# FFN products as two streams of 64 array rows, one on w_in and one on w_out

## The chip, the cores and the metric

The kernel runs on one core of one Trainium2 chip. A core has five engines that run side by side, each through its own instructions in order: TensorE (PE, matrix products into the accumulation memory PSUM), VectorE (DVE) and ScalarE (ACT) for elementwise work, GpSimd (POOL), and SyncE (SP), which here issues the DMA transfers. The profile counts TensorE's loads of stationary operands as an engine of their own, PEld. PSUM has eight banks; a bank holds 128 partitions x 512 float32. The metric is the time of one execution on the device in microseconds (us); lower is better.

## The reference, cut to what matters

Two parts follow each other. The first is attention with decay over 4 sequences of 768 tokens, 8 heads of 64. The second takes its result, 3072 tokens x 512, through a feed-forward network (FFN) whose nonlinearity is a ratio of two polynomials:

```python
for t in range(S):
    state = gamma * state + einsum('bhd,bhe->bhde', k[:, :, t], v[:, :, t])
    y[:, :, t] = scale * einsum('bhd,bhde->bhe', q[:, :, t], state)
x = y.transpose(0, 2, 1, 3).reshape(3072, 512)
h = x @ w_in                                  # 512 -> 2048
P = a[0] + a[1] * h + a[2] * h * h + a[3] * h * h * h
Q = 1.0 + abs(b[0]) * abs(h) + abs(b[1]) * h * h
out = (P / (Q + 1e-06)) @ w_out               # 2048 -> 512
```

## The kernel before, in words

**Blocks and slots.** The tokens are cut into 6 blocks of 512. Attention makes a block as four chunks of 128 tokens. The 2048 hidden features are cut into 16 tiles of 128. A *slot* is one pair (block n, feature tile f); `order` lists the 96 of them: blocks 0 and 1 with tiles 0 to 7, both again with tiles 8 to 15, then blocks 2 to 5 with 16 tiles each. Each FFN operand is held as a rounded high part and a low part, and a product takes three terms: high x high, high x low, low x high.

**One slot on PE.** `gemm_in` (L346) makes h for the slot in one PSUM bank `ph` (two banks take turns) with 12 products: three terms by four parts of the 512 input features, each contracting over all 128 rows of the array, 512 columns. `gemm_out` (L398) takes the slot that is three behind (`LAG = 3`), with its g = P/Q split into `gh` and `gl`, and adds into four banks `po`, one for each 128 tokens, with 12 products more: four token tiles by three terms. A group of slots (all 16 tiles of a block, or 8 for blocks 0 and 1) accumulates in the same four banks. When the group is done, `store` (L422) empties the banks: copies, two by ACT and two by DVE (L431), or, for the second half of blocks 0 and 1, four additions by DVE (L428); the next group uses the same banks.

**One slot on the other engines.** `poly_scalar` (L362) reads ph on ACT (Abs, L366; two affine maps, L372 and L374; in some slots the first of them is POOL's L368) and multiplies on POOL (L373). `poly_vector` (L377) finishes P on DVE, reading ph (L378, L379). `ratio_scalar` (L382) makes 1/Q on ACT by a reciprocal square root (L383) and Square (L384), which is written over ph. `ratio_vector` (L386) refines it and multiplies on DVE (L387 to L389), with ph as scratch. In the next iteration `split` (L391) makes gh on ACT (L394) and gl on POOL (L395).

**Weights** come packed. `decode_read` (ACT, L128 and L136), `decode_join` (DVE, L144 and L147), `decode_split` (high part, ACT, L157) and `decode_rest` (low part, POOL, L164) unpack one tile of w_in or w_out in a slot, 32 tiles in all up to slot 24. The list `tiles` sets their order: w_in is four tiles ahead of w_out, and the last four decoded, in slots 21 to 24, are tiles 12 to 15 of w_out.

**Attention** for block n runs between the FFN products while block n-1 is worked on. The dictionary `parts` names the slots: part 0 of a chunk makes the scores (L226, pairs of 64-row products in two banks) and their mask (L235); part 1 makes the state's update, the recall and the values (L247, L260, L271) and puts x into its high and low parts (L295, L299). Block 1 has slots 0 to 7, block 2 slots 24 to 31, the others every second slot of the 16 before their block.

**Order.** `run` (L456) writes the order of all four compute engines by hand, and no planner changes it. In iteration k it issues: in(k), Abs and the rest of poly(k), split(k-1), the late decoding steps, attention's part 1, out(k-3), store, attention's part 0, decoding, ratio(k). DMA issues stand on SP in the order of the program.

The lines that set the order around the change:

```python
            if k < nslot:
                mid[k] = poly_scalar(gemm_in(*order[k]), plain)
...
                poly_vector(*mid[k])
            if 0 < k <= nslot:
                g[k - 1] = split(mid.pop(k - 1)[1])
...
            if k >= LAG:
                n, f = order[k - LAG]
                gemm_out(n, f, *g.pop(k - LAG))
                if groups[n, f][1]:
                    store(n, None if n >= 2 else f // HF)
```

Of the kernel before, what the change touches and what calls it, by code (L numbers as in the profile page):

```python
# [7 lines left out]
F32 = mybir.dt.float32  # L8
# [4 lines left out]
AF = mybir.ActivationFunctionType  # L13
ALU = mybir.AluOpType
PSUM = bass.MemoryType.PSUM

P = 128
# [4 lines left out]
def tile_retention_rational_ffn(  # L22
# [15 lines left out]
    nc = tc.nc  # L38
    B, C = qT.shape[0], qT.shape[1]
    H, D = kk.shape[3], kk.shape[4]  # L40
    NP = H // 2
    NF = w_in.shape[0]
    DM = out.shape[1]
    NSTEP = B * C
    SPB = TB // P
# [4 lines left out]
    at = ctx.enter_context(tc.tile_pool(name="at", bufs=2))  # L50
    ff = ctx.enter_context(tc.tile_pool(name="ff", bufs=2))
    ps_o = ctx.enter_context(tc.tile_pool(name="ps_o", bufs=1, space=PSUM))
# [3 lines left out]
    o_tiles = {}  # L56
# [31 lines left out]
    par_sb = const.tile([P, 6], F32, name="par_sb")  # L88
    babs = const.tile([P, 2], F32, name="babs")
    qcon = const.tile([P, 1], F32, name="qcon")  # L90
# [4 lines left out]
    w1, w2 = {}, {}  # L95
# [3 lines left out]
    lead, HF = 4, NF // 2  # L99
    tiles = []  # L100
# [6 lines left out]
    def fetch(count=1):  # L107
        for m, f in tiles[len(raws) : len(raws) + count]:
            raw = wp.tile([P, DM, 2], U32, name="raw", tag=f"w{m}_{f}")
            nc.sync.dma_start(  # L110
                out=raw.rearrange("p m w -> p (m w)"), in_=(w_in, w_out)[m][f]
            )
            raws.append(raw)
# [3 lines left out]
    def decode_read(i):  # L117
        decode_low(i)
        decode_high(i)
# [48 lines left out]
    x_tiles = {}  # L168
# [39 lines left out]
    def scale_v(i):  # L208
        st = steps[i]
        nc.gpsimd.tensor_mul(  # L210
            st["v"], st["v"], vdec_sb.unsqueeze(2).broadcast_to([P, H, D])
        )
# [95 lines left out]
    def opening():  # L308
# [3 lines left out]
        def fill(n):  # L312

            for _ in range(n):
                nc.tensor.matmul(idle, zeros[:, :P], zeros, start=True, stop=True)

        fill(FILL[0])
        scale_v(0)
# [4 lines left out]
        for i in range(SPB):  # L323
            outer(i)
            recall(i)
            fill(FILL[1])
            values(i)
# [51 lines left out]
        nc.vector.scalar_tensor_tensor(p, p, par_sb[:, 1:2], ph, ALU.add, ALU.mult)  # L379


    def ratio_scalar(ph, p, q, s):  # L382
        nc.scalar.activation(s, q, AF.Abs_reciprocal_sqrt, bias=qcon[:, 0:1])  # L383
        nc.scalar.activation(ph, s, AF.Square)  # L384

    def ratio_vector(ph, p, q, s):  # L386
        nc.vector.scalar_tensor_tensor(q, q, qcon[:, 0:1], ph, ALU.add, ALU.mult)  # L387
        nc.vector.scalar_tensor_tensor(ph, p, par_sb[:, 0:1], ph, ALU.add, ALU.mult)  # L388
        nc.vector.scalar_tensor_tensor(p, q, 2.0, ph, ALU.subtract, ALU.mult, reverse0=True)  # L389

    def split(p):  # L391
        gh = ff.tile([P, TB], F32R, name="gh", bufs=BUFS["gh"])
# [2 lines left out]
        nc.gpsimd.tensor_sub(gl, p, gh.bitcast(F32))  # L395
        return gh, gl

    def gemm_out(n, f, gh, gl):  # L398
        first, last = groups[n, f]
        if first:  # L400
            o_tiles[n] = [ps_o.tile([P, DM], F32, name="po", tag=f"po{i}") for i in range(SPB)]
        terms = ((gh, 0), (gh, 1), (gl, 0))


        pairs = [(m, tt) for m in range(3) for tt in range(SPB)]
        if first or last:
            pairs = [(m, tt) for tt in range(SPB) for m in range(3)]
        for m, tt in pairs:
            g_, part = terms[m]
            nc.tensor.matmul(  # L410
                o_tiles[n][tt], g_[:, tt * P : (tt + 1) * P], w2[f][:, part],
                start=(first and m == 0), stop=(last and m == 2),
            )

    halves, sums = {}, {}

# [5 lines left out]
    def store(n, half):  # L422
# [16 lines left out]
    order = [(n, f) for h in range(2) for n in range(2) for f in range(h * HF, (h + 1) * HF)]  # L439
    order += [(n, f) for n in range(2, NB) for f in range(NF)]  # L440
    nslot = len(order)
    groups = {
        (n, f): (f == 0 or (n < 2 and f == HF), f == NF - 1 or (n < 2 and f == HF - 1))
        for n, f in order
    }
# [3 lines left out]
    parts = {}  # L449
    for n in range(1, NB):  # L450
        end = order.index((n, 0))
        begin = {1: 0, 2: 3 * HF}.get(n, end - NF)
        for a in range(2 * SPB):
            parts[begin + a * (end - begin) // (2 * SPB)] = (SPB * n + a // 2, a % 2)

    def run():  # L456

        mid, g, waiting, resting = {}, {}, [SPB], []
        for k in range(nslot + LAG):
            fetch(min(len(tiles), FETCH + 2 * k) - len(raws))  # L460
            chunk, part = parts.get(k, (None, None))

            tile_ = SPB + 2 + k + (k > 1)
            if k == LAG - 1:
                opened.append(k)
            plain = part is None and tile_ < len(tiles)
            if plain and tile_ not in ts:
                decode_read(tile_)
            if k < nslot:
                mid[k] = poly_scalar(gemm_in(*order[k]), plain)  # L470
                if k == 0:
                    decode_join(SPB + 1)
                    waiting.append(SPB + 1)
                poly_vector(*mid[k])
# [7 lines left out]
            if part == 1:  # L482
                outer(chunk)
                recall(chunk)
                values(chunk)
            if k >= LAG:
                n, f = order[k - LAG]
                gemm_out(n, f, *g.pop(k - LAG))
                if groups[n, f][1]:
                    store(n, None if n >= 2 else f // HF)  # L490
            if k + 1 >= LAG and k + 1 - LAG < nslot:
                n, f = order[k + 1 - LAG]
# [8 lines left out]
            if k < nslot:  # L501
                ratio_scalar(*mid[k])
# [67 lines left out]
FETCH = 13  # L570
FIRST = (1, 1, 1, 1, 3, 1)
LAG = 3
FILL = (10, 2)


# [56 lines left out]
```

## Time and profile before

| | |
|---|---|
| time, median of three runs | 645.76 us (644.24 to 646.43) |
| span of the profiled execution, first to last instruction | 642.4 us |
| mean granted TensorE clock in it | 0.994 of full speed |
| busy: PE, PEld, DVE, ACT, POOL | 620.0, 498.2, 460.1, 441.7, 334.1 us |
| FFN products: on w_in (L355), on w_out (L410) | 1164 and 1152 |

A row of a timeline gives the start in us from the span's beginning, the length, the engine, the line, the operation, output<-inputs, the shape of the array tile (for PE, rows*columns), the operands' shapes, and xN where N like instructions in a row are drawn together; in brackets, how long the engine had been idle and what ended that. The end of a product is modelled, its start is measured. A table by stage gives the stretch, its length, the busy time of PE, PEld, DVE, ACT and POOL with the number of instructions, then the granted clock, the DMA share and GB/s. "L366 <-PE ph L355" reads: the instruction of line 366 was released by the product of line 355 that writes ph.

### The profile page before, as it was taken

Reading aid. Unit: us, or ns where it says so; the run is one execution under the profiler, and the core shown is the slowest. Engines: PE = TensorE matmul, PEld = TensorE weight load, DVE = VectorE, ACT = ScalarE, POOL = GpSimd, SP = SyncE. Lnnn points to the kernel's source line nnn. Section 1 sums busy time; section 2 is a strip of 40 time slices with the busy share of each in tenths; the row PEclk is TensorE's granted clock in tenths of the full one; section 3 lists DMA queues with packets and bytes.
Section 4 is the critical chain, followed back from the end, with each engine's and each line's share of the span. In section 5 each row is a group of like instructions: output and inputs, shape, how many; then the busy total and the mean of one; then the engine's idle time right before and its main releaser. Section 6 shows DMA issues by size and latency. Waiting matters only on the chain.

```text
span 642.4 us, 10022 instructions
## 1 busy us (share of the span) xinstructions
PE 620.0 (97%) x3739; PEld 498.2 (78%) x3742; DVE 460.1 (72%) x731; ACT 441.7 (69%) x721; POOL 334.1 (52%) x288
## 2 busy tenths in 40 slices
PE   8777999999999999999999999999999999999997
PEld 5555778888877778788888878878888888888885
DVE  3788788888888666767676676667766766666664
ACT  2687889889885556566656575766666666777773
POOL 2566668887874434444544453535354434444442
PEclk9988999999999999999999999999999999999999
DMA  8984572001033222310110321001311000010001
GB/s 316 400 331 167 201 252 109 1 1 65 1 121 127 66 67 82 132 51 17 49 50 17 115 51 50 34 21 54 108 33 35 1 0 1 26 41 2 1 1 65
DMA packets 24384, 52.36 MB, mean 82 GB/s; under 512 B 3088, under 2 KB 3216, under 8 KB 24336
## 3 DMA queue, kind: packets, MB, share of 16 engines
q1 hardware_dynamic: 24336, 51.73, 23.4%
q8 instruction: 29, 0.48, 0.3%
q14 instruction: 19, 0.16, 0.1%
HBM read 43.33 MB, written 8.39 MB: 81 GB/s over the span
## 4 chain that ended last, share of the span: by engine, by line
PE 85%; DMA 4%; ACT 4%; DVE 3%; issue 2%; SPq 1%; POOL 0%; POOLq 0%; DVEq 0%; ACTq 0%
PE ph L355 38%; PE po L410 38%; PE px L271 3%; PE pa L226 3%; DMA v<-in_v 1%; PE px L260 1%; PE px L247 1%; DMA qT<-in_qT 1%; DMA k<-in_k 1%; DMA xdec_sb<-in_xdec 1%; ACT s L372 1%; SPq L192 1%; DVE o L428 1%; ACT t L128 1%; ACT q L366 1%
## 5 line engine op out<-in xcount | busy, mean ns | idle before, releaser
L373 POOL TENSOR_TENSOR q<-q,s 128x512 f32<-128x512 f32 x96 | 124.3, 1295 | 228.0 <-ACT s L372 217.9
L355 PE MATMUL ph<-xh,w 128*128 128x512 f32 (+2 forms) x776 | 210.3, 393 | 8.4 <-DVE p L389 4.8
L410 PE MATMUL po<-w,gh 128*128 128x512 f32 x768 | 200.2, 393 | 0.0
L355 PEld LDWEIGHTS ph<-xh,w 128*128 128x128 f32 x776 | 143.9, 188 | 41.5 <-DVE t L147 2.8
L410 PEld LDWEIGHTS po<-w,gh 128*128 128x128 f32 x768 | 142.9, 188 | 32.4 <-ACT p L374 1.5
L366 ACT ACTIVATE q<-ph 128x512 f32<-128x512 f32 x96 | 57.2, 596 | 118.6 <-PE ph L355 118.5
L378 DVE TENSOR_TENSOR p<-ph,p 128x512 f32<-128x512 f32 x96 | 66.2, 690 | 94.3 <-ACT p L374 94.3
L395 POOL TENSOR_TENSOR gl<-p,gh 128x512 fp32r<-128x512 f32 x96 | 124.3, 1295 | 8.9 <-ACT gh L394 3.6
L410 PE MATMUL po<-w,gl 128*128 128x512 f32 x384 | 110.5, 389 | 0.2 <-POOL gl L395 0.2
L387 DVE SCALAR_TENSOR_TENSOR q<-q,qcon,ph 128x512 f32<-128x512 f32 x96 | 71.4, 744 | 47.0 <-ACT ph L384 46.8
L355 PE MATMUL ph<-xl,w 128*128 128x512 f32 (+2 forms) x388 | 103.9, 390 | 0.0
L383 ACT ACTIVATE s<-q,qcon 128x512 f32<-128x512 f32 x96 | 69.4, 722 | 22.5 <-POOL q L373 22.5
L355 PEld LDWEIGHTS ph<-xl,w 128*128 128x128 f32 x388 | 72.8, 188 | 15.3
L410 PEld LDWEIGHTS po<-w,gl 128*128 128x128 f32 x384 | 72.1, 188 | 15.6 <-POOL gl L395 0.6
L379 DVE SCALAR_TENSOR_TENSOR p<-p,par_sb,ph 128x512 f32<-128x512 f32 x96 | 71.8, 748 | 3.4
L374 ACT ACTIVATE p<-ph,par_sb 128x512 f32<-128x512 f32 x96 | 73.1, 761 | 0.0
L388 DVE SCALAR_TENSOR_TENSOR ph<-p,par_sb,ph 128x512 f32<-128x512 f32 x96 | 72.0, 750 | 0.0
L394 ACT CAST gh<-p 128x512 fp32r<-128x512 f32 x96 | 58.8, 613 | 15.9 <-DVE p L389 15.9
L389 DVE SCALAR_TENSOR_TENSOR p<-q,ph 128x512 f32<-128x512 f32 x96 | 65.9, 687 | 3.3
L372 ACT ACTIVATE s<-q,babs 128x512 f32<-128x512 f32 x80 | 65.3, 817 | 2.7
L384 ACT ACTIVATE ph<-s 128x512 f32<-128x512 f32 x96 | 57.8, 602 | 10.0 <-DVE p L379 0.8
L210 POOL TENSOR_TENSOR v<-v,vdec_sb 128x512 f32<-128x512 f32 x24 | 25.0, 1044 | 43.9 <-DMA v<-in_v 43.9
(37 smaller groups left out, 446.2 us busy)
## 6 DMA issues: line engine op xcount, KB each, us to landing
raw<-in_w_in SPq DMA_DIRECT2D x16, 512.0 KB, 5.4
raw<-in_w_out SPq DMA_DIRECT2D x16, 512.0 KB, 7.4
kT<-in_kT SPq DMA_DIRECT2D x24, 256.0 KB, 2.8
qT<-in_qT SPq DMA_DIRECT2D x24, 256.0 KB, 3.0
v<-in_v SPq DMA_DIRECT2D x24, 256.0 KB, 3.5
out<-o SPq DMA_DIRECT2D x24, 256.0 KB, 2.2
k<-in_k SPq DMA_DIRECT2D x20, 256.0 KB, 3.7
half<-o SPq DMA_DIRECT2D x8, 256.0 KB, 2.2
```

Source lines behind the costliest of these rows:

```text
L355: nc.tensor.matmul(ph[:, t0:t1], w1[f][:, part, kt * P : (kt + 1) * P], x[:, kt, t0:t1], start=(i == 0), stop=(i == 3 * NP - 1),)
L372: nc.scalar.activation(s, q, AF.Identity, bias=babs[:, 0:1], scale=babs[:, 1:2])
L373: nc.gpsimd.tensor_mul(q, q, s)
L374: nc.scalar.activation(p, ph, AF.Identity, bias=par_sb[:, 2:3], scale=par_sb[:, 3:4])
L378: nc.vector.tensor_mul(p, ph, p)
L379: nc.vector.scalar_tensor_tensor(p, p, par_sb[:, 1:2], ph, ALU.add, ALU.mult)
L383: nc.scalar.activation(s, q, AF.Abs_reciprocal_sqrt, bias=qcon[:, 0:1])
L387: nc.vector.scalar_tensor_tensor(q, q, qcon[:, 0:1], ph, ALU.add, ALU.mult)
L388: nc.vector.scalar_tensor_tensor(ph, p, par_sb[:, 0:1], ph, ALU.add, ALU.mult)
L389: nc.vector.scalar_tensor_tensor(p, q, 2.0, ph, ALU.subtract, ALU.mult, reverse0=True)
L395: nc.gpsimd.tensor_sub(gl, p, gh.bitcast(F32))
L410: nc.tensor.matmul(o_tiles[n][tt], g_[:, tt * P : (tt + 1) * P], w2[f][:, part], start=(first and m == 0), stop=(last and m == 2),)
```

## The change: what it does

From slot 10 (`SPLIT`) on, each FFN product over 128 array rows is written as two over 64: the upper stream uses rows 0 to 63, the lower one rows 64 to 127. In a slot the upper stream does its 12 half products on w_in, then its 12 on w_out; the lower stream does w_out first, then w_in, three products behind the upper one (`BEHIND`). PE's instructions alternate between the two. So at any time the streams write different banks; where they change places, a PE instruction without work (`after`) waits until the other stream has left the bank. The bank ph of slot k is complete with the lower stream's last product, which is issued after the first three of the upper stream in slot k+1; attention's products of iteration k follow, then the rest of slot k+1. The output products of slot k (for the feature tile of slot k-3) start with the lower stream's first product of the slot.

The slots after the last in(k) (out of the last three) and slots 0 to 9 stay as they were. From slot 10 on, Square and the ratio's intermediate go to the SBUF tile `s` and not to ph. Attention for block 2 starts in slot 22 and has ten slots in place of eight.

```diff
-    def ratio_scalar(ph, p, q, s):
+    def ratio_scalar(y, p, q, s):
         nc.scalar.activation(s, q, AF.Abs_reciprocal_sqrt, bias=qcon[:, 0:1])
-        nc.scalar.activation(ph, s, AF.Square)
+        nc.scalar.activation(y, s, AF.Square)
-    def ratio_vector(ph, p, q, s):
+    def ratio_vector(y, p, q, s):
...
+    def after(earlier):
+        tc.add_manual_dep(
+            nc.tensor.nop().ins, earlier.ins.name,
+            mybir.DependencyInfo(mybir.DependencyClass.Sync, mybir.DependencyReason.DATA),
+            reason="row tiles take turns at a bank",
+        )
...
+    def product_in(k, r, i):
+        n, f = order[k]
+        if r == 0 and i == 0:
+            made[k, "ph"] = bank("ph")
+        if r == 1 and i == 0:
+            after(made[k, "in", 0, TERMS - 1])
+        part, x, kt = ([(0, 0)] * NP + [(0, 1)] * NP + [(1, 0)] * NP)[i] + (i % NP,)
+        rows = slice(r * P // 2, (r + 1) * P // 2)
+        made[k, "in", r, i] = nc.tensor.matmul(
+            made[k, "ph"], w1[f][rows, part, kt * P : (kt + 1) * P], x_tiles[n][x][rows, kt],
+            start=(r == 0 and i == 0), stop=(r == 1 and i == TERMS - 1),
+        )
+
+    def product_out(k, r, i):
+        n, f = order[k - LAG]
+        first, last = groups[n, f]
+        tt, m = divmod(i, 3)
+        g_, part = ((g[k - LAG][0], 0), (g[k - LAG][0], 1), (g[k - LAG][1], 0))[m]
+        if r == 1 and i == 0:
+            out_banks(n, first)
+            if (k - 1, "out", 0, TERMS - 1) in made:
+                after(made[k - 1, "out", 0, TERMS - 1])
+        if r == 0 and i % 6 == 0:
+            after(made[k, "out", 1, i + 5])
+        rows = slice(r * P // 2, (r + 1) * P // 2)
+        made[k, "out", r, i] = nc.tensor.matmul(
+            o_tiles[n][tt], g_[rows, tt * P : (tt + 1) * P], w2[f][rows, part],
+            start=(first and r == 1 and m == 0), stop=(last and r == 0 and m == 2),
+        )
+
+    def upper(k, s):
+        (product_in if s < TERMS else product_out)(k, 0, s % TERMS)
+
+    def lower(k, s):
+        (product_out if s < TERMS else product_in)(k, 1, s % TERMS)
+
+    def gemm_both(k):
+        for s in range(0 if k == SPLIT else BEHIND, 2 * TERMS):
+            upper(k, s)
+            if s >= BEHIND:
+                lower(k, s - BEHIND)
+        for s in range(BEHIND):
+            if k + 1 < nslot:
+                upper(k + 1, s)
+            lower(k, 2 * TERMS - BEHIND + s)
+        g.pop(k - LAG)
+        return made[k, "ph"]
...
-        begin = {1: 0, 2: 3 * HF}.get(n, end - NF)
+        begin = {1: 0, 2: 3 * HF - 2}.get(n, end - NF)
...
-            if k < nslot:
+            both = SPLIT <= k < nslot
+            if both:
+                mid[k] = poly_scalar(gemm_both(k), plain)
+                poly_vector(*mid[k])
+                mid[k] = (mid[k][3], *mid[k][1:])
+            elif k < nslot:
...
-                gemm_out(n, f, *g.pop(k - LAG))
+                if not both:
+                    gemm_out(n, f, *g.pop(k - LAG))
                 if groups[n, f][1]:
                     store(n, None if n >= 2 else f // HF)
...
+SPLIT = 10
+BEHIND = 3
+TERMS = 12
```

More of the change, by code (lines that the diff above doesn't have):

```diff
@@ L379, in poly_vector @@
         nc.vector.scalar_tensor_tensor(p, p, par_sb[:, 1:2], ph, ALU.add, ALU.mult)
-    def ratio_scalar(ph, p, q, s):
+    def ratio_scalar(y, p, q, s):
         nc.scalar.activation(s, q, AF.Abs_reciprocal_sqrt, bias=qcon[:, 0:1])
-        nc.scalar.activation(ph, s, AF.Square)
-    def ratio_vector(ph, p, q, s):
-        nc.vector.scalar_tensor_tensor(q, q, qcon[:, 0:1], ph, ALU.add, ALU.mult)
-        nc.vector.scalar_tensor_tensor(ph, p, par_sb[:, 0:1], ph, ALU.add, ALU.mult)
-        nc.vector.scalar_tensor_tensor(p, q, 2.0, ph, ALU.subtract, ALU.mult, reverse0=True)
+        nc.scalar.activation(y, s, AF.Square)
+    def ratio_vector(y, p, q, s):
+        nc.vector.scalar_tensor_tensor(q, q, qcon[:, 0:1], y, ALU.add, ALU.mult)
+        nc.vector.scalar_tensor_tensor(y, p, par_sb[:, 0:1], y, ALU.add, ALU.mult)
+        nc.vector.scalar_tensor_tensor(p, q, 2.0, y, ALU.subtract, ALU.mult, reverse0=True)
     def split(p):
@@ L396, in split, with out_pairs @@
         return gh, gl
[L398 to L402, printed above, removed]
+    def out_pairs(first, last):
         pairs = [(m, tt) for m in range(3) for tt in range(SPB)]
@@ L407, in gemm_out, with out_banks @@
             pairs = [(m, tt) for tt in range(SPB) for m in range(3)]
-        for m, tt in pairs:
+        return pairs
+    def out_banks(n, first):
+        if first:
+            o_tiles[n] = [ps_o.tile([P, DM], F32, name="po", tag=f"po{i}") for i in range(SPB)]
+        return o_tiles[n]
+    def gemm_out(n, f, gh, gl):
+        first, last = groups[n, f]
+        po = out_banks(n, first)
+        terms = ((gh, 0), (gh, 1), (gl, 0))
+        for m, tt in out_pairs(first, last):
             g_, part = terms[m]
@@ L410, in gemm_out @@
             nc.tensor.matmul(
-                o_tiles[n][tt], g_[:, tt * P : (tt + 1) * P], w2[f][:, part],
+                po[tt], g_[:, tt * P : (tt + 1) * P], w2[f][:, part],
                 start=(first and m == 0), stop=(last and m == 2),
             )
+    def after(earlier):
[4 more added lines that the diff above has]
+        )
@@ new lines, in tile_retention_rational_ffn @@
+    made, g = {}, {}
+    def product_in(k, r, i):
[10 more added lines that the diff above has]
+        )
@@ new lines, in product_out @@
+    def product_out(k, r, i):
+        n, f = order[k - LAG]
+        first, last = groups[n, f]
+        tt, m = divmod(i, 3)
[11 more added lines that the diff above has]
+        )
@@ L456, in run @@
     def run():
-        mid, g, waiting, resting = {}, {}, [SPB], []
+        mid, waiting, resting = {}, [SPB], []
         for k in range(nslot + LAG):
```

## The prediction

> **What bounds the kernel now.** I read the page first (span, busy times, the chain that ended last), then the timeline of PE for the pace of its products, then the timelines of ACT, DVE and POOL in three slots, because the change moves the moment at which their work is released.
>
> ```profile
> span 642.4 us, 10022 instructions
> ...
> PE 620.0 (97%) x3739; PEld 498.2 (78%) x3742; DVE 460.1 (72%) x731; ACT 441.7 (69%) x721; POOL 334.1 (52%) x288
> ...
> PE ph L355 38%; PE po L410 38%; PE px L271 3%; PE pa L226 3%; DMA v<-in_v 1%; PE px L260 1%; PE px L247 1%; DMA qT<-in_qT 1%; DMA k<-in_k 1%; DMA xdec_sb<-in_xdec 1%; ACT s L372 1%; SPq L192 1%; DVE o L428 1%; ACT t L128 1%; ACT q L366 1%
> ```
>
> The two FFN lines are 76% of the chain, so PE's pace sets the time. The chain's own rows give that pace, and the timeline of PE gives the ends of the stage that the change rewrites: the first product of slot 10, and the first product behind slot 95's last ph product.
>
> ```profile
> 284.12 2.72 PE ph L355 x12
> ...
> 292.28 2.72 PE po L410 x12
> ...
> 101.05 1.07 PE L355 MATMUL ph<-xh,w 128*128 128x512 f32 x4
> ...
> 627.20 1.98 PE L410 MATMUL po<-w,gh 128*128 128x512 f32 x8
> ```
>
> From 284.12 to 292.28 lie 36 products: 8.16/36 = 0.2267 us each, 5.44 us a slot. From 101.05 to 627.20 there are 526.15 us with 85 x 24 + 12 = 2052 products, 465.2 us of them; the other 61.0 us are attention and waits. Behind 627.20 follow 15.2 us.
>
> **The gain: a pair of 64-row products.** PE's timeline has 512-column FFN products in a stage with half the granted clock (quoted with the clock below), and 64-row products in pairs (scores, L226), early at a slow pace and later at full clock:
>
> ```profile
> 35.19 1.91 PE L355 MATMUL ph<-xh,w 128*128 128x512 f32 x4
> 36.47 0.63 PE L355 MATMUL ph<-xh,w 128*128 128x512 f32 x1
> ...
> 5.94 1.35 PE L226 MATMUL pa<-qT,kT 64*128 64x128 f32 x14
> 6.58 0.71 PE L226 MATMUL pa<-qT,kT 64*128 64x128 f32 x8
> ...
> 295.14 0.95 PE L226 MATMUL pa<-qT,kT 64*128 64x128 f32 x14
> 295.81 0.28 PE L226 MATMUL pa<-qT,kT 64*128 64x128 f32 x2
> ```
>
> The row at 36.47 is the fourth product of the row at 35.19: 1.28/3 = 0.427 at half clock, so 0.2135 at full clock is array time, and 0.2267 - 0.2135 = 0.013 is something the faster clock does not shorten. For the score pairs (x14 to x8 is three pairs, x14 to x2 six) it is 0.64/3 = 0.213 slow and 0.67/6 = 0.1117 fast: array 0.1067, rest 0.005, though these are two streams, each with its own weights. That the early pace is the half clock I infer from the pace: the view records no clock there. The change makes each full product one such pair. Bounds of a pair: 0.2135 (nothing but array time) and 0.2267 (both streams keep today's 0.013). The nearest row is the score pair, so I take 0.2135 + 0.005 = 0.2185.
>
> The Trainium skill (TensorE: Matmul & The Clock Gate, Measured speedup vs the span model) puts a second row tile at about 4 ns above one product; on 0.2135 that would be 0.2175 and 2 us less in the sum than mine, on 0.2267 it would be 0.2307, which speaks against any gain. No run here shows 512-column pairs.
>
> The sum so far, against the execution with the 642.4 span: 86 slots of 24 pairs, and three pairs at slot 10 where the upper stream runs alone, are 2067 pairs. Slot 95's ph product now ends with the whole slot, so only out(93) and out(94) lie between it and out(95). That end is tied to gl, not to PE:
>
> ```profile
> 634.79 1.29 POOL L395 TENSOR_TENSOR gl<-p,gh 128x512 fp32r<-128x512 f32 x1 [3.31 <-issue]
> 636.14 0.50 PE L410 MATMUL po<-w,gl 128*128 128x512 f32 x1 [0.17 <-POOL gl L395]
> ```
>
> PE waits for gl at 636.14 today, 8.94 after 627.20, so the 15.2 us stay, with a longer hole before. Total: 101.05 + 61.0 + 15.2 + 2067 x 0.2185 = 628.9, or 13.5 less than 642.4. At 0.2267 it would be 645.9, since out(92) no longer hides in the tail.
>
> **The loss: what slot k+1's output products wait for.** Today slot k+1 runs in(k+1) first, so out starts 5.44 us after ph(k) is complete. After the change the lower stream's first instruction behind ph(k)'s last one is slot k+1's first w_out product; only slot k's attention products stand between. ACT, DVE and POOL run in written order, and all that they do in iteration k stands behind Abs(ph(k)), L366. A slot without decoding shows how long that takes; X = 501.89 is the first PE start behind the last ph product:
>
> ```profile
> 501.89 1.98 PE L410 MATMUL po<-w,gh 128*128 128x512 f32 x8
> 502.09 0.60 ACT L366 ACTIVATE q<-ph 128x512 f32<-128x512 f32 x1 [2.44 <-PE ph L355]
> ...
> 503.62 1.30 POOL L373 TENSOR_TENSOR q<-q,s 128x512 f32<-128x512 f32 x1 [4.23 <-ACT s L372]
> ...
> 504.11 0.61 ACT L394 CAST gh<-p 128x512 fp32r<-128x512 f32 x1
> ...
> 504.88 1.30 POOL L395 TENSOR_TENSOR gl<-p,gh 128x512 fp32r<-128x512 f32 x1
> ...
> 504.97 0.75 DVE L379 SCALAR_TENSOR_TENSOR p<-p,par_sb,ph 128x512 f32<-128x512 f32 x1
> ```
>
> Three uses of these rows are harmless. ph's bank is free with L379 at X + 3.83; its next writer comes 21 pairs, 4.59, behind X. gl(k-1) is done at X + 4.29 and wanted at X + 5.24 + 0.44. Both covers are under 1.5 us: an engine later than that would stall PE by the excess. The four added waits of a slot are 3.5 to 4 pairs (0.76 to 0.87) behind the product waited for, which lasts 0.39 (1.07 less three steps at 101.05); nothing else is queued behind them but PE's own stream.
>
> Two uses are not harmless: stores and decoded weights. Slots in which these stand (store with copies, store with adds, and a decoded tile's low half behind gl):
>
> ```profile
> 149.37 0.62 ACT L394 CAST gh<-p 128x512 fp32r<-128x512 f32 x1 [0.51 <-DVE p L389]
> 149.90 1.07 ACT L431 COPY o<-po 128x512 f32<-128x512 f32 x2
> ...
> 149.98 0.75 DVE L379 SCALAR_TENSOR_TENSOR p<-p,par_sb,ph 128x512 f32<-128x512 f32 x1
> 150.64 1.28 DVE L431 COPY o<-po 128x512 f32<-128x512 f32 x2
> ...
> 199.35 1.88 DVE L428 TENSOR_TENSOR o<-po,o 128x512 f32<-128x512 f32 x3
> ...
> 139.62 1.29 POOL L395 TENSOR_TENSOR gl<-p,gh 128x512 fp32r<-128x512 f32 x1
> 140.88 1.30 POOL L164 TENSOR_TENSOR w<-t,w 128x512 fp32r<-128x512 f32 x1
> ...
> 102.60 1.30 POOL L164 TENSOR_TENSOR w<-t,w 128x512 fp32r<-128x512 f32 x1
> ```
>
> *Stores.* A finished group's four po banks are emptied in iteration k (L431, L428), behind gh; the next group starts in slot k+1 on the same banks. ACT's first copy starts 0.53 behind gh's start and takes about 0.54, so bank 0 is free at X + 2.22 + 1.07 = X + 3.3; PE restarts 0.16 later (0.05 behind gl at 636.14, and 0.11 more than a usual first product). DVE's first copy starts 0.66 behind L379's start and frees bank 1 at X + 3.08 + 0.66 + 0.64 = X + 4.4, wanted three pairs behind bank 0. Together 3.9 us of standing PE; with adds (0.62 each, all on DVE) X + 4.36 + 0.16 = 4.5. If the first product waited for all four banks it would be 5.2. Slots hit: 11, 19 and 83 at 3.9; 27 (adds) 4.5; 35 (adds), 51 and 67 have slot k's attention in front.
>
> The cover by attention comes from the starts of slots 74 to 77:
>
> ```profile
> 504.62 1.07 PE L355 MATMUL ph<-xh,w 128*128 128x512 f32 x4
> ...
> 512.51 1.07 PE L355 MATMUL ph<-xh,w 128*128 128x512 f32 x4
> ...
> 517.96 1.07 PE L355 MATMUL ph<-xh,w 128*128 128x512 f32 x4
> ...
> 524.58 1.19 PE L355 MATMUL ph<-xh,w 128*128 128x512 f32 x4
> ```
>
> 7.89, 5.45 and 6.62: a slot with part 1 is 2.44 longer, one with part 0 is 1.17 longer. So slot 35 loses 4.5 - 2.44 = 2.1, slots 51 and 67 1.4 each.
>
> *Weights.* w_out tiles 12 to 15 are decoded in slots 21 to 24, their low halves (L164) come behind gl in iterations 22 to 25, and slots 23 to 26 multiply by them: ready at X + 2.99 + 2.56 = X + 5.55, with the restart 5.7, wanted one pair after the attention: 5.7 - 1.17 - 0.22 = 4.3 in slots 23 and 25, 5.7 - 2.44 - 0.22 = 3.0 in slots 24 and 26, 14.6 in all. Tile 7 is ready at 103.90 and wanted at 101.05 + 4 pairs = 101.92: 2.1 in slot 10.
>
> Sum: 2.1 + 3 x 3.9 + 4.5 + 2.1 + 2 x 1.4 + 14.6 = 37.8 us.
>
> *The clock.* Standing PE also loses clock (the table by stage, PE busy first, granted clock last but two):
>
> ```profile
> 32.71 0.50 PE L355 MATMUL ph<-xh,w 128*128 128x512 f32 x1 [2.62 <-DVE t L147]
> ...
> 30.68:34.09 3.41, 1.38 (x6) 1.14 (x7) 2.69 (x4) 3.38 (x6) 2.58 (x3) 1.00 1.02 408
> 34.10:37.50 3.40, 3.40 (x16) 2.26 (x16) 2.64 (x4) 3.37 (x7) 3.40 (x3) 0.50 1.03 405
> 37.52:40.92 3.40, 2.01 (x44) 1.53 (x42) 2.88 (x5) 2.36 (x4) 1.30 (x2) 1.00 0.96 332
> 40.92:44.33 3.41, 2.74 (x12) 2.17 (x12) 3.00 (x7) 2.82 (x6) 2.09 (x2) 1.00 0.92 331
> ```
>
> A stretch with PE busy 1.38 of 3.41 us is followed by one at 0.50; one with 2.01 of 3.40 is not. A hole of 3 to 4.5 us leaves some such stretch mostly empty. The price is at most 1.7 us a time; I take 1.3, since part of the slow stretch falls into the hole, and seven of the eight holes from 3.0 us up: 9 us (0 to 15).
>
> *Other edits.* Ratio's scratch in SBUF: Square writes SBUF as the 0.61 us cast gh does; the three DVE instructions change their second operand's place, for which before has no row: as DVE stands free behind the ratio in most slots, I take nothing, -0.1 to +0.1 us in each of 12 decoding slots. Attention of block 2 two slots earlier: the same work, and it is why slots 23 to 26 have that cover.
>
> Sum: 628.9 + 37.8 + 9 = 675.7, that is 33.3 over the span. The three runs stand 1.8 to 4.0 over that span, their median 3.4, so 679.
>
> **Rivals.** *The pairs gain nothing* (0.2267): 645.9 + 47 + 3.4 = 696. For it: each stream is as long as today's, and the score pairs have 128 columns of another type. Against it: their 0.005.
>
> *POOL and DVE shut each other out in the decoding slots.* The ratio now reads two SBUF tensors in three DVE instructions:
>
> ```profile
> 142.86 0.77 POOL L368 TENSOR_SCALAR s<-q,babs 128x512 f32<-128x512 f32 x1 [0.69 <-ACT q L366]
> ...
> L387 DVE SCALAR_TENSOR_TENSOR q<-q,qcon,ph 128x512 f32<-128x512 f32 x96 | 71.4, 744 | 47.0 <-ACT ph L384 46.8
> ```
>
> If they and POOL's four (0.77 + 3 x 1.30 = 4.67) could never overlap, a decoding slot would need 4.67 + 3 x 0.74 = 6.9 instead of 5.24; over nine such slots that have no store or weight wait, 15 us more: 694. Before has no DVE instruction with two SBUF tensors, so its rows can't decide. The Trainium skill (SBUF — State Buffer, Who interferes with whom) says that such an instruction and a GpSimd one that reads SBUF lock each other out; by that rule this rival holds.
>
> *Faster.* The holes do not open, because the banks and low halves come free before ph(k) is complete: the first copy needs only slot k's own w_out products, which end 12 pairs before ph(k), and ACT stands idle then (2.44 us before 502.09). Were copies and subtractions queued ahead of Abs, the sum would be 628.9 + 3.4 = 632; it turns the sign where less than 13.5 us of holes and clock remain. Against it: copies stand behind gh, and gh behind Abs, in every row above.
>
> *The streams do not overlap at all*: 2067 x 0.2267 more, some 1145.
>
> **How the numbers follow.** Forecast 0.55, pairs without gain 0.15, shut-out 0.12, faster 0.11, no overlap 0.02; 0.05 is left for holes half as large (655). The range goes from small holes with little clock loss (half of 47 saved: 655, and 650 with pairs at 0.2135) to the pairs without gain with long holes (702): 650 to 702. Faster by over 0.3% (about what a measurement of this kernel can tell from no change) 0.12, within 0.02, slower 0.86.
>
> **What would show it.** Pairs: L-rows of FFN products 64*128 whose pairs start 0.2185 apart. Holes: PE idle before the first w_out products of slots 11, 19, 27 and 83, released by the L431 and L428 instructions, of 3.5 to 4.5 us; in slots 23 to 26 released by L164's low halves; granted clock 0.5 in stretches behind them. The shut-out would show as longer DVE or POOL rows in the decoding slots. The forecast is wrong if the holes sum to under 14 us, or the pair step is 0.2267 or more.

## The result, and the profile after

The changed kernel takes 696.62 us (median of four runs, 695.95 to 698.96), the kernel before 645.87 beside it (644.24 to 646.43): ratio 1.0797, 95% interval 1.0771 to 1.0823. It is slower by 8%. The profiled execution has a span of 694.2 us against 642.4, so 51.8 us are to be accounted for. The page of the changed kernel, with the span, the busy times, the chain by line and the costliest group (busy us, mean ns | idle before it and what ended most of that):

```profile
span 694.2 us, 14125 instructions
...
PE 638.0 (92%) x5803; PEld 524.2 (76%) x5806; DVE 481.8 (69%) x731; ACT 445.2 (64%) x723; POOL 342.5 (49%) x286
...
PE po L455 32%; PE ph L438 30%; PE po L415 3%; PE ph L355 2%; PE px L271 2%; PE pa L226 2%; POOL q L373 1%; POOL gl L395 1%; POOL w L164 1%; DVE p L389 1%; DMA raw<-in_w_out 1%; DVE q L387 1%; PE px L260 1%; DMA v<-in_v 1%; DMA qT<-in_qT 1%
...
L455 PE MATMUL po<-w,gh 64*128 64x512 f32 x1376 | 383.8, 400 | 33.2 <-POOL w L164 11.4
```

L438 is the half product on w_in, L455 the one on w_out; L498 is what L431 was before (copies of a store), L495 what L428 was (additions). PE still carries most of the chain, but its share of the span fell from 97% to 92%, while 18.0 us of busy time were added, a part of them at half clock (below): nothing here speaks for a gain in PE's work, and there are holes in it.

**The pace.** Rows of the chain that ended last, in the last slots, where nothing disturbs PE (start, length, line, like products drawn together):

```profile
619.70 0.91 PE po L455 x8
...
625.14 0.91 PE po L455 x8
...
630.58 0.91 PE po L455 x8
```

From 619.70 to 625.14 and on to 630.58 are 5.44 us a slot, and a slot has 24 pairs: 0.2267 each, the same as a full product before. The pair gains nothing.

**A hole.** The timeline of slot 83, which starts the products of a new group in banks that the last group's store empties:

```profile
601.93 0.60 ACT L366 ACTIVATE q<-ph 128x512 f32<-128x512 f32 x1 [1.19 <-PE ph L438]
...
603.94 0.60 ACT L394 CAST gh<-p 128x512 fp32r<-128x512 f32 x1
...
604.45 1.07 ACT L498 COPY o<-po 128x512 f32<-128x512 f32 x2
...
605.08 0.62 PE L455 MATMUL po<-w,gh 64*128 64x512 f32 x1 [2.97 <-ACT o L498]
...
605.50 0.62 PE L455 MATMUL po<-w,gh 64*128 64x512 f32 x1
```

The copy stands behind gh, gh behind Abs, and Abs waits for ph(k), as the prediction had it. PE stands for 2.97 us and then runs at half pace (605.08 to 605.50 is 0.42 a pair). The waits of PE, in total us, number and longest:

```profile
PE po L455 <- POOL w L164: 11.4, 6, 5.0
PE po L455 <- ACT o L498: 11.0, 5, 4.6
PE po L455 <- DVE o L495: 6.8, 2, 4.3
```

**The clock.** The table by stage (length, busy time of PE, PEld, DVE, ACT and POOL, granted clock, DMA share, GB/s):

```profile
101.60:184.80 83.20, 73.32 (x580) 59.02 (x581) 63.19 (x84) 56.11 (x96) 58.41 (x47) 0.94 0.07 26
184.80:253.39 68.59, 50.73 (x433) 38.83 (x431) 39.72 (x60) 32.07 (x54) 28.52 (x23) 0.85 0.18 58
253.39:601.70 348.31, 344.44 (x3448) 282.56 (x3445) 246.93 (x377) 227.79 (x362) 160.96 (x133) 1.00 0.16 48
601.72:612.06 10.34, 7.37 (x50) 5.83 (x49) 6.18 (x9) 4.80 (x8) 2.50 (x2) 0.83 0.27 103
612.06:677.70 65.64, 65.64 (x577) 65.16 (x573) 42.46 (x59) 47.39 (x72) 30.64 (x24) 1.00 0.01 1
```

Slots 10 to 21 (first row), 22 to 27 (second) and 83 (fourth) have most of the holes, and the granted clock falls there. Together the three rows are short of full clock by 0.06 x 83.2 + 0.15 x 68.6 + 0.17 x 10.3 = 17 us; a part of that lies in the holes themselves. The third row, slots 28 to 82, has holes too (slots 35, 51 and 67) and keeps the full clock: PE's 2.49 us of idle time before 302.47, in slot 35, are followed by no half clock.

**The decoding slots.** A third loss is in slots 14 to 18, which last 5.76 to 6.13 us in place of 5.44. The timeline of ACT, DVE and POOL in one of them:

```profile
142.49 1.30 POOL L164 TENSOR_TENSOR w<-t,w 128x512 fp32r<-128x512 f32 x1
...
143.38 0.95 DVE L387 SCALAR_TENSOR_TENSOR q<-q,qcon,s 128x512 f32<-128x512 f32 x1 [0.55 <-ACT s L384]
...
144.37 0.75 DVE L388 SCALAR_TENSOR_TENSOR s<-p,par_sb,s 128x512 f32<-128x512 f32 x1
144.38 1.30 POOL L368 TENSOR_SCALAR s<-q,babs 128x512 f32<-128x512 f32 x1 [0.60 <-ACT q L366]
145.16 1.06 DVE L389 SCALAR_TENSOR_TENSOR p<-q,s 128x512 f32<-128x512 f32 x1
```

L387 ends at 144.33, 0.54 behind POOL's L164 (143.79). L368 took 0.77 before and takes 1.30 here, ending 0.56 behind L388 (145.12). L389 ends 0.54 behind L368 (145.68). Whichever of the two engines is first holds the other back. The Trainium skill (SBUF — State Buffer, Who interferes with whom) says that a DVE instruction with two SBUF inputs and a GpSimd instruction that reads SBUF exclude each other; these rows agree.

**A gain in the scores.** The timeline of PE at a block of score products (L226) between FFN products, in the kernel before:

```profile
522.49 1.07 PE L410 MATMUL po<-w,gl 128*128 128x512 f32 x4
523.49 1.16 PE L226 MATMUL pa<-qT,kT 64*128 64x128 f32 x16
524.58 0.73 PE L355 MATMUL ph<-xh,w 128*128 128x512 f32 x2
```

And in the changed kernel:

```profile
565.43 1.07 PE L438 MATMUL ph<-xh,w 64*128 64x512 f32 x7
566.33 1.05 PE L226 MATMUL pa<-qT,kT 64*128 64x128 f32 x16
567.14 0.47 PE L438 MATMUL ph<-xh,w 64*128 64x512 f32 x1
```

From the first score product to the next FFN product are 1.09 us before and 0.81 after. Over the two slots that a block touches the traces have 6.62 + 5.58 before and 6.25 + 5.54 after: 0.41 less, in 16 blocks 6.6 us. The scores' array tile is 64*128, and now the FFN's is too; that this is the cause is a reading of the rows, which no run changes by itself. A full block of part 1, whose tiles differ in shape from the FFN's in both kernels, costs 2.46 in both, which agrees.

### The profile page after: what moved, and what is told of

It is laid out like the page before. It is cut to its first block, busy times and chain, and to the rows that moved or that the text cites. A ratio compares the mean times of both kernels' runs of the same rounds, so it can differ in the third digit from the quotient of the medians.

```text
span 694.2 us, 14125 instructions
## 1 busy us (share of the span) xinstructions
PE 638.0 (92%) x5803; PEld 524.2 (76%) x5806; DVE 481.8 (69%) x731; ACT 445.2 (64%) x723; POOL 342.5 (49%) x286
## 4 chain that ended last, share of the span: by engine, by line
PE 74%; ACT 7%; DVE 5%; DMA 5%; POOL 4%; issue 4%; SPq 1%; POOLq 0%; DVEq 0%; ACTq 0%
PE po L455 32%; PE ph L438 30%; PE po L415 3%; PE ph L355 2%; PE px L271 2%; PE pa L226 2%; POOL q L373 1%; POOL gl L395 1%; POOL w L164 1%; DVE p L389 1%; DMA raw<-in_w_out 1%; DVE q L387 1%; PE px L260 1%; DMA v<-in_v 1%; DMA qT<-in_qT 1%
## 5 line engine op out<-in xcount | busy, mean ns | idle before, releaser
L455 PE MATMUL po<-w,gh 64*128 64x512 f32 x1376 | 383.8, 400 | 33.2 <-POOL w L164 11.4
L438 PE MATMUL ph<-xh,w 64*128 64x512 f32 x1376 | 305.6, 394 | 1.4 <-DVE p L379 1.4
L455 PEld LDWEIGHTS po<-w,gh 64*128 64x128 f32 x1376 | 235.1, 190 | 64.0 <-POOL w L164 13.9
L455 PE MATMUL po<-w,gl 64*128 64x512 f32 x688 | 247.4, 396 | 0.0
L438 PEld LDWEIGHTS ph<-xh,w 64*128 64x128 f32 x1376 | 208.9, 187 | 28.2 <-DVE p L379 3.4
L438 PE MATMUL ph<-xl,w 64*128 64x512 f32 x688 | 191.6, 397 | 0.0
L438 PEld LDWEIGHTS ph<-xl,w 64*128 64x128 f32 x688 | 127.8, 187 | 10.1
L455 PEld LDWEIGHTS po<-w,gl 64*128 64x128 f32 x688 | 122.4, 190 | 12.5
L387 DVE SCALAR_TENSOR_TENSOR q<-q,qcon,s 128x512 f32<-128x512 f32 x86 | 69.5, 808 | 34.5 <-ACT s L384 33.7
L379 DVE SCALAR_TENSOR_TENSOR p<-p,par_sb,ph 128x512 f32<-128x512 f32 x96 | 71.8, 748 | 3.4
L388 DVE SCALAR_TENSOR_TENSOR s<-p,par_sb,s 128x512 f32<-128x512 f32 x86 | 70.1, 815 | 3.0
L394 ACT CAST gh<-p 128x512 fp32r<-128x512 f32 x96 | 58.5, 610 | 17.5 <-DVE p L389 17.4
L389 DVE SCALAR_TENSOR_TENSOR p<-q,s 128x512 f32<-128x512 f32 x86 | 63.0, 733 | 3.0
```

Of the source, the lines that this page charges most:

```text
L387: nc.vector.scalar_tensor_tensor(q, q, qcon[:, 0:1], y, ALU.add, ALU.mult)
L388: nc.vector.scalar_tensor_tensor(y, p, par_sb[:, 0:1], y, ALU.add, ALU.mult)
L389: nc.vector.scalar_tensor_tensor(p, q, 2.0, y, ALU.subtract, ALU.mult, reverse0=True)
L438: made[k, "in", r, i] = nc.tensor.matmul(made[k, "ph"], w1[f][rows, part, kt * P : (kt + 1) * P], x_tiles[n][x][rows, kt], start=(r == 0 a ...
L455: made[k, "out", r, i] = nc.tensor.matmul(o_tiles[n][tt], g_[rows, tt * P : (tt + 1) * P], w2[f][rows, part], start=(first and r == 1 and ...
```

## The experiments

**The step of a product, by itself.** The question was whether a pair of half products can run in less than 0.2267 us, and what the 0.013 above the array time belongs to. The kernel leaves out attention and FFN and fills its output with an input; it runs series of products in bfloat16 (bf16), in the FFN's rounded float32 type (float32r), and in float32, full or as pairs of halves (a comment behind # gives the line in the profile and what the series is):

```diff
+            for i in range(25):
+                mm(full, wr[:, 0], xr, **one)                       # L70: float32r, same weights each time
+            for i in range(25):
+                mm(full, wb[:, i % NP], xb, **one)                  # L72: bf16
...
+            for i in range(25):
+                mm(up, wr[half[0], i % NP], xr[half[0]], **one)     # L78: one stream of halves alone
+            for i in range(50):
+                mm(banks[i % 2], wr[half[i % 2], i // 2 % NP], xr[half[i % 2]], **one)       # L80: pairs
...
+            for i in range(25):
+                mm(full[:, :P], w32[:, i % NP], x32[:, :P], **one)  # L86: float32, 128 columns
...
+            for i in range(50):
+                mm(banks[i % 2][:, :P], w32[half[i % 2], i // 2 % NP], x32[half[i % 2], :P], **one)   # L90
```

> Products alone, no attention and no FFN: loops of 25 products or 25 pairs with nothing else on the core; the output is filled with one of the inputs. Start to start, after the first few. Prediction's step (what is over array time is per pair, 0.005): 64-row pairs of float32r, 512 columns, 0.2185 a pair, against 0.2267 for full products. Theory after the trace (what is over array time, 0.0133, belongs to each float32r stream by itself): full 0.2267, one 64-row stream alone 0.2267, a pair 0.2267; 256 columns 0.120 in both forms; bf16 some 0.216 in both forms; float32 pairs of 128 columns 0.1117 per pair and half instruction as in the scores. If it is the weights' load that disturbs the stream, weights of 64 columns give about 0.220 and the same weights again and again change nothing; if it is the moving operand, 64 columns of weights give 0.2267.

Its timeline of PE in the float32r and bf16 products:

```profile
23.58 5.83 PE L70 MATMUL full<-xr,wr 128*128 128x512 f32 x25
29.48 5.34 PE L72 MATMUL full<-xb,wb 128*128 128x512 bf16 x24
...
49.29 0.39 PE L80 MATMUL up<-xr,wr 64*128 64x512 f32 x1
49.42 0.39 PE L80 MATMUL low<-xr,wr 64*128 64x512 f32 x1
...
52.46 0.39 PE L80 MATMUL up<-xr,wr 64*128 64x512 f32 x1
...
52.69 0.39 PE L80 MATMUL low<-xr,wr 64*128 64x512 f32 x1
```

And its timeline of PE in the float32 products, where the two rows of L86 are one series, cut at two points:

```profile
64.32 0.50 PE L86 MATMUL full<-x,w 128*128 128x128 f32 x3
64.32 3.85 PE L86 MATMUL full<-x,w 128*128 128x128 f32 x33
...
91.00 0.27 PE L90 MATMUL up<-x,w 64*128 64x128 f32 x1
...
92.90 0.27 PE L90 MATMUL up<-x,w 64*128 64x128 f32 x1
```

Full float32r products are (5.83 - 0.39)/24 = 0.2267 apart, though their weights never change; bf16 products of the same size (5.34 - 0.38)/23 = 0.2157. In the pairs of halves, 14 steps lie between the two rows of the upper stream (0.2264 each) and 14 between those of the lower one (0.2336, while it falls back from 0.67 to 0.44 us ahead of the upper one; at the end both step alike). One stream alone steps at 0.227, full float32r products of 256 columns at 0.120, those with weights of 64 columns at 0.230. Twice the step of 256 columns less that of 512 leaves 0.0133 too. So a float32r product takes about 0.013 above its array time at full clock, with 64 rows as with 128, with 256 columns as with 512, with new weights or the same ones. Each stream of halves is as long as the full one was, and nothing of the 0.013 is hidden behind the other.

The rows of L86 settle what the prediction read from the score pairs: full float32 products of 128 columns are (3.85 - 0.50)/30 = 0.1117 apart, and pairs of halves 1.90/17 = 0.1118. The score pairs' small remainder belongs to the data type, not to the pairing. The Trainium skill (TensorE: Matmul & The Clock Gate, Measured speedup vs the span model) adds about 4 ns for a second row tile. That would be 0.1 us in a slot of 24 pairs, and the FFN's 5.44 us a slot shows none of it.

This run also has borders between series of the same type. From the last 128*128 product of L88 (90.16) to the first 64*128 one of L90 (90.68) are 0.52 us, where L88 steps at 0.43, and from 128*64 (L76, 43.16) to 64*128 (L78, 43.48) 0.32, where L76 steps at 0.23. Where the shape of the array tile stays, L86 to L88 (69.01 to 69.12) and L90 to L92, the step is L86's and L90's own 0.11. So these two changes of shape cost 0.09 us each, while one from 128*128 to 128*64 (L74 at 37.53, L76 at 37.65) cost nothing. A score block has two borders; at 0.09 each they would make up 0.18 of its 0.41 by this estimate, and the rest stays open.

**Stores ahead of Abs.** The copies and additions of a finished group are issued before ph(k) is waited for:

```diff
-                mid[k] = poly_scalar(gemm_both(k), plain)
+                ph = gemm_both(k)
+                n, f = order[k - LAG]
+                if groups[n, f][1]:
+                    store(n, None if n >= 2 else f // HF)
+                mid[k] = poly_scalar(ph, plain)
...
-                if groups[n, f][1]:
+                if groups[n, f][1] and not both:
```

> The changed kernel, with a finished group's four stores issued between gemm_both(k) and poly_scalar(k), ahead of Abs(ph(k)); nothing else. Theory (holes): ACT and DVE stand idle before Abs, so the banks come free in time and the holes at slots 11, 19, 27, 35, 51, 67 and 83 go. These slots were longer than their neighbours by 4.7, 7.1, 7.3, 2.8, 1.3, 1.3 and 4.9 us in the changed kernel's trace (29.4 with the half clock behind them); some 3 us come back because more of the decoding slots then run at their own 6.1 us: 670 (665 to 675). Rival (the banks were not what the output products waited for): no change, 697.

Measured: 673.7 us, ratio 1.0439 [1.0411, 1.0467], 22.9 us less than the changed kernel. Slots 11, 27 and 35 fall to 5.44, 6.25 and 5.89 (from 10.12, 13.53 and 8.32), slots 51 and 67 to 5.57: the store's place was the cause there. Two holes stay, in slot 19 and, smaller, in slot 83. Its timeline there:

```profile
158.25 0.60 ACT L157 CAST w<-t 128x512 fp32r<-128x512 f32 x1
...
158.76 1.06 ACT L498 COPY o<-po 128x512 f32<-128x512 f32 x2
...
159.39 0.79 PE L455 MATMUL po<-w,gh 64*128 64x512 f32 x1 [1.56 <-ACT o L498]
...
584.03 0.69 DVE L389 SCALAR_TENSOR_TENSOR p<-q,s 128x512 f32<-128x512 f32 x1
...
584.64 1.28 DVE L498 COPY o<-po 128x512 f32<-128x512 f32 x2
...
585.38 0.50 PE L455 MATMUL po<-w,gh 64*128 64x512 f32 x1 [0.97 <-DVE o L498]
```

In slot 19 ACT comes to the copies late, behind a decoding slot's cast; in slot 83 DVE's copies stand behind the ratio of the slot before. Moving the store ahead of Abs puts it behind the work before Abs, which is late wherever the engines are. The half clock lasts 6.8 us in slot 19 here too (0.50 from 159.2 to 166.0), although its waits for copies, 1.56 and 0.51, are much shorter than in the changed kernel (4.63).

**Weights ahead of Abs.** The late decoding steps, the high half on ACT and the low half on POOL, are issued before ph(k) is waited for:

```diff
-                mid[k] = poly_scalar(gemm_both(k), plain)
+                ph = gemm_both(k)
+                while waiting:
+                    decode_split(waiting[0])
+                    resting.append(waiting.pop(0))
+                while resting:
+                    decode_rest(resting.pop(0))
+                mid[k] = poly_scalar(ph, plain)
```

> The changed kernel, with the late decoding steps (high half on ACT, low half on POOL) issued between gemm_both(k) and poly_scalar(k), ahead of Abs(ph(k)); nothing else. Theory (holes): slots 23 to 26, which were longer than their kind by 7.8, 2.8, 7.0 and 2.8 us with the half clock behind them, fall to their kind: 696.6 - 20.4 = 676 (671 to 681). Rival: the low halves were not the last thing waited for, and the first output product of these slots stays late: 690 or more.

Measured: 688.43 us, ratio 1.0681 [1.0657, 1.0705]; the expectation is missed by 12 us, and the rival's 690 is not reached either. Slots 23 to 26 fell from 47.85 us together to 35.05, that is by 12.8 of the 20.4 expected: the weights' place cost that much, and the rest goes to other waits, as of the scores in slot 24 for L147 (2.46). Slots 14 to 18 went up to 6.7 to 6.9 us, and slot 19 stayed at 13.47. In slot 35 the same wait as in the changed kernel, 2.49 us for the additions, is followed by 3.4 us of half clock here (0.50 from 295.80 to 299.21) and by none there: the length of a hole alone does not decide.

**Both ahead of Abs.**

> Both of the moves: stores and late decoding ahead of Abs(ph(k)). Theory: what is left over the kernel before is the three lone products and the longer tail (3.4 us at 0.2267 a pair), the hole in slot 10 (1.7), some ten decoding slots at 6.1 in place of 5.44 us (7), less 0.4 us for each of some 14 chunks of attention, whose scores no longer change the array's mode (5.7): 645.9 + 6.4 = 652 (648 to 656). Rival (the holes hide a second wait of like size behind them, on gl or on ph's bank): 665 or more. Second rival (a pair gains something once nothing waits): under 645.

Its edit is the two edits above. Measured: 670.07 us, ratio 1.0397 [1.0377, 1.0417], where the theory had 652 and the rival, that a second wait takes the place of the first, 665 or more: the rival held. From slot 28 on the slots are as the theory has them; before that they are not. Its timeline in a decoding slot:

```profile
142.15 1.41 POOL L164 TENSOR_TENSOR w<-t,w 128x512 fp32r<-128x512 f32 x1 [1.36 <-ACT w L157]
142.45 1.67 DVE L388 SCALAR_TENSOR_TENSOR s<-p,par_sb,s 128x512 f32<-128x512 f32 x1
143.56 1.20 POOL L368 TENSOR_SCALAR s<-q,babs 128x512 f32<-128x512 f32 x1
144.15 1.15 DVE L389 SCALAR_TENSOR_TENSOR p<-q,s 128x512 f32<-128x512 f32 x1
...
146.73 1.19 PE L438 MATMUL ph<-xh,w 64*128 64x512 f32 x7 [1.12 <-DVE p L379]
```

The low half now meets the ratio on DVE: L388 is held from 142.45 to 144.12, 0.56 behind L164's end, and everything behind it comes later, up to L379, which sets ph's bank free for PE. In slot 19 PE waits for the copies again (1.56 and 2.37). In slots 22 to 25 of this kernel, which last 8.2 to 10.6 us, PE's waits are for ph's bank (0.84 us, ended by L379), for a low half (0.78, L164) and, before the scores in slot 24, for L147 (2.62), which reads a bank that the scores take next, and 1.31 us before L247 have no releaser in the profile; how these came about was not taken apart further.

**The scratch alone.** The kernel before, with full products, and only the ratio's scratch in SBUF from slot 10 on:

```diff
-    def ratio_scalar(ph, p, q, s):
+    def ratio_scalar(y, p, q, s):
...
-        nc.scalar.activation(ph, s, AF.Square)
+        nc.scalar.activation(y, s, AF.Square)
...
+                if k >= SPLIT:
+                    mid[k] = (mid[k][3], *mid[k][1:])
```

> The kernel before, full 128-row products throughout, with only ratio's scratch moved from ph to the SBUF tile s from slot 10 on. Shut-out theory (a DVE instruction with two SBUF tensors and a POOL instruction wait for each other): the decoding slots 10 to 23 go from 5.44 to about 6.1 us, as in the changed kernel's slots 14 to 18, with L368 and L387 to L389 lengthened there and nowhere else: some 14 x 0.66 = 9 us, 655 (651 to 657). Rival (those 6.1 us came from the streams and their hold on ph): no change, 645.9.

Measured: 652.7 us, ratio 1.0136 [1.012, 1.0152]: 8.0 us for an edit that the prediction costed at nothing. The size is as expected, the place is not. The period of the other engines in the decoding slots, from one L394 to the next, goes from 5.36 to 6.11 us, but PE's slots stay at 5.44 until the lead of three slots is used up, and then PE stands twice. Its page has for POOL's first map, which took 772 ns before:

```profile
L368 POOL TENSOR_SCALAR s<-q,babs 128x512 f32<-128x512 f32 x16 | 19.0, 1190 | 12.9 <-ACT q L366 12.9
```

And its timeline of PE has the two holes:

```profile
156.80 0.73 PE L410 MATMUL po<-w,gh 128*128 128x512 f32 x2 [2.82 <-ACT o L431]
...
184.58 1.45 PE L410 MATMUL po<-w,gh 128*128 128x512 f32 x4 [3.05 <-POOL w L164]
```

A stretch at half clock follows each (0.50 from 158.05 to 161.45 and from 185.36 to 188.75), and the kernel before has neither hole: 5.9 us of standing and up to 1.7 us for each slow stretch are enough for the 8 us.

In the changed kernel the lead is shorter, as ph(k) is complete half a slot later, and from slot 14 on PE waits for ph's bank in every decoding slot.

**Filled holes.** To price the clock by itself, PE gets 14 bf16 products on zeros ahead of the holes of slots 27 and 83, into a bank that nobody reads:

```diff
+                if k + 1 in (27, 83):
+                    idle = bank("idle")
+                    for _ in range(14):
+                        nc.tensor.matmul(idle, zeros[:, :P], zeros, start=True, stop=True)
```

> The changed kernel with 14 products on zeros (3.0 us) issued on PE ahead of the output products of slots 27 and 83, in the time in which they wait for the stores. Theory (a hole costs twice: its own length and the half clock behind it): slot 83 falls from 10.34 to about 8.6 us with the clock at full speed behind it, slot 27 from 13.5 to about 11.5, although PE has more to do. Rival (the half clock is the consequence of something else): both stay as they are or grow.

One execution took 689.8 us, span 688.0 against 694.2, although work was added. The table by stage over the hole of slot 83 and what follows, in the changed kernel:

```profile
601.72:605.30 3.58, 0.61 (x5) 0.22 (x4) 2.54 (x4) 3.34 (x6) 1.85 (x2) 1.00 0.02 5
605.31:608.72 3.41, 3.41 (x18) 2.46 (x18) 3.18 (x6) 1.46 (x3) 0.64 (x1) 0.50 0.70 266
```

And in this one, the stretch with the filling products and the next:

```profile
598.24:601.44 3.20, 3.15 (x16) 1.36 (x15) 2.16 (x4) 3.05 (x6) 1.57 (x2) 1.00 0.00 0
601.45:603.60 2.15, 2.09 (x15) 1.53 (x17) 1.99 (x4) 1.75 (x4) 0.95 (x1) 1.00 0.38 147
```

Without the standing, there is no half clock. Slots 82 and 83 together take 14.59 us in place of 15.78, slots 26 and 27 19.16 in place of 21.84. The other engines are no faster for it, so these 1.2 and 2.7 us are the clock's: these two holes cost their length and then that, more where the half clock lasted twice as long (6.8 us at slot 27's hole). They are 3.9 of the 6.2 us between the two spans; the rest lies elsewhere, and one execution does not show that the filling made it.

**Where the streams pay.** If pairs gain nothing but the scores between them do, the streams should run only where scores stand and no hole opens: from slot 34 to 79, with the stores ahead of Abs and attention's block 2 back in its old slots. The second kernel keeps the streams to slot 95.

```diff
-SPLIT = 10
+SPLIT = 34
+END = 80
...
-            both = SPLIT <= k < nslot
+            both = SPLIT <= k < END
```

> The changed kernel with stores ahead of Abs, streams in slots 34 to 79 alone (no decoding there, and old products in the tail), attention of block 2 back in slots 24 to 31. Theory: a pair costs what a full product costs, so the streams gain only at the scores, whose products have the same shape of array tile: a slot with scores and the one behind it took 6.25 + 5.54 against 6.62 + 5.58 before, 0.4 us for each of 11 chunks, less the three lone pairs (0.7): 645.0 - 3.8 = 641 (640 to 643). Rival (scores gained because attention waited less, not by the shape): no change, 645 or more.

> As the run with streams in slots 34 to 79, but with the streams up to slot 95 as in the change. Theory: nothing in slots 80 to 95 gains, and the tail loses the 2.7 us of out(92), which now stands ahead of the end of in(95), and a longer hole before gl(95): 644 (643 to 646). Rival: the tail costs nothing: 641.

Measured: 641.0 us for slots 34 to 79, ratio 0.9949 [0.9935, 0.9963]: 3.7 us below the kernel before beside it (644.73), and the fastest of all kernels here. With slots 80 to 95 as well 644.91, ratio 1.0001 [0.9987, 1.0014]. The two-stream form is worth about half a per cent through the scores, and loses that again where no scores follow: slot 83 is 1.26 us longer there for a hole, and the output products of one slot, out(92), no longer hide in the tail (2.7 us by the expectation). The times show that the gain belongs to the slots with scores; they do not separate the tile's shape from other causes.

## Why the prediction was right and wrong

It forecast 679 us, slower, in a range of 650 to 702; 696.62 lies in the range. The direction is owed to the holes, which opened as forecast. The range holds the time because its upper end was drawn for the rival *the pairs gain nothing*; by the prediction's own sign ("or the pair step is 0.2267 or more") the forecast's mechanism was wrong in its gain. The lower end of 650 does not follow from its working either: half of the 47 saved and pairs at 0.2135 give 655 - 10 = 645. The sum of its steps, against the measured parts of the span, in us:

| part | predicted | measured |
|---|---|---|
| 2067 pairs | x 0.2185 = 451.6 | x 0.2267 = 468.5 |
| ends before and behind the pairs | 101.05 + 15.2 = 116.2 | 101.6 + 16.5 = 118.1 |
| holes | 37.8 | 38.0 |
| clock behind the holes | 9 | 14.8 |
| decoding slots 14 to 18 | 0 | 3.0 |
| attention and small waits | 61.0 | 51.8 |
| span | 675.7 | 694.2 |

The holes are the 22 starts of PE in slots 10, 11, 19, 23 to 27, 35, 51, 67 and 83 that come over 0.5 us behind the start before them, 43.0 us together, less one step of 0.2267 each. The clock is what these slots' lengths have beyond a slot's 5.44, its attention and the holes; the table by stage allows 17 for it.

**The step that failed is the gain.** The pair's 0.2185 was made of 0.2135 array time and 0.005 from the score pairs. Measured are 0.2267, the upper bound, and that alone moves the sum by 16.9 of the 18.5 us that it missed. The score pairs are float32 with 128 columns; the 0.005 was taken for a property of pairs and is one of float32 products, full ones included (0.1117 against 0.1118). The prediction had the reason for doubt in the rival's favour ("the score pairs have 128 columns of another type") and still gave that rival 0.15. That rival's time of 696 is the one measured; that it came so close is in part luck, as its other terms were off as well, in both directions: clock, decoding slots and ends by 10.7 us too low, attention by 9.2 too high.

**The holes were right in mechanism**, and their sum is so close in part by luck, as the errors one by one cancel: slots 11 and 83 lost 2.8 and 3.1 where 3.9 was forecast, slots 19 and 23 lost 5.2 and 5.5 where 3.9 and 4.3 was. In slot 19 the engines were late from the decoding slots before it, a delay that the working did not carry on from slot to slot; slot 35 lost 2.8 and not 2.1.

**The clock was undersized.** The term had 1.3 us for each of seven holes from one half-clock stretch of 3.4 us. Six holes had a half clock: it lasted 6.8 us at those of slots 19, 23, 25 and 27, where it began within the hole or between two, and 3.4 at those of slots 11 and 83. The holes of slots 24, 26 and 35, of 2.7 to 2.8 us, had none.

**The scratch in SBUF was costed at nothing, and was not nothing.** Its rival had the mechanism right; its price of 15 us took DVE's and POOL's instructions for never overlapping at all. By itself the scratch costs 8.0 us, in the changed kernel 3.0 in slots 14 to 18 and, not measured apart, a part of slot 19's hole.

**Attention was taken as unchanged** ("slot k's attention products stand between" with their old prices). The scores save 6.6 us where their tile shape is the FFN's; the other 2.6 us of that row are waits of the kernel before. Three of them make up most of it: PE stands 0.53 and 0.54 us before L247 (187.81, 203.08) and 1.11 before L355 (270.44), which the 61.0 counted with attention and the changed kernel does not have. This gain hid the undersized clock and the scratch from the total.

**The rival "faster" did not hold** even with its own cure: with copies and subtractions ahead of Abs the kernel takes 670.07, not 632. Of the 38 us between, 17 are the pairs. The rest lies mostly in slots 13 to 25: in 13 to 18, some 8.5 us, the moved work meets DVE and POOL, and the waits in the others are those named above, whose origin is open. Its statement that the first copy needs only products that end 12 pairs before ph(k) is right for the first bank alone: in slot 82 that bank's last product starts at 598.78 and the last product of ph(k) at 601.50, but the last bank's starts at 600.82, three pairs ahead, as the upper stream does its part of w_out last.

## What to carry to other kernels

A remainder above the array time belongs to the type and size of the product in which it was measured: price a new form of product from a row of the same type, or measure the step alone, before a gain is built on it. When work is reordered so that a product starts where the old one had a slot of lead, list what that lead was hiding (stores, late weights, banks) and look for what is queued ahead of each; a hole can then be paid twice, in length and in clock. Moving scratch from PSUM to SBUF lengthens the rows of DVE and POOL that meet (0.77 to 1.30 us here), and where slots have a lead, the delay is paid only where the lead ends.

## What the runs showed of the hardware that was not expected

- At full clock a float32r product takes about 13 ns above its array time, a bf16 product of the same size about 2: 0.2267 against 0.2157 for 512 columns. 64 rows in place of 128, new weights and pairing don't change it. At half clock no such remainder shows: from 605.08 to 608.50 pairs are 0.4275 apart, about twice the array time of 0.2134 (0.2267 less 0.0133).
- Score blocks between half products of the same array tile shape cost 0.41 us less than between full products. Among products alone, two changes of the tile's shape cost 0.09 us each, a third nothing; what the rest of the 0.41 is stays open.
- The two streams are not in step. In the slots behind 612 us each lower product starts 0.18 us behind the upper one that is issued with it, and each stream keeps its 0.2267.
- The half clock came in stretches of 3.4 or 6.8 us, and the length of a hole alone does not set which: in the changed kernel 6.8 at slots whose holes sum to over 4.6 us (19, 23, 25, 27) and 3.4 at slots 11 and 83 with 2.8 and 3.1, but none at slot 35 with 2.8; with the stores ahead 6.8 at slot 19 with shorter waits; with the weights ahead 3.4 at slot 35.
